# Attention output and decayed receptance transposed by DMA instead of TensorE, in an RWKV-6 and HyperMixer kernel

## The chip, the cores and the metric

The kernel runs on one core of a Trainium2 chip. The metric is the device time of one execution in microseconds; lower is better. Each execution is also put in a state: "slow" when it is over 1.5% above the fastest execution of the same kernel, else "fast". Ratios and their 95% intervals use fast executions alone.

The views name the engines PE (TensorE; PEld are its weight loads), DVE (VectorE), ACT (ScalarE), POOL (GpSimd) and SP (SyncE, which issues most of the DMA transfers here); SPq and ACTq are what SP and ACT issue. In this kernel TensorE writes its products to the memory PSUM, and DVE or ACT copies them out: that copy is an eviction. The granted clock is the share of its full clock that TensorE was given. A transfer is issued, and later it lands.

## The reference

Inputs and output are float32, with B = 4 batches, H = 8 heads, S = 768 positions and D = 48 channels a head. A linear attention with decay feeds a token mixer:

```python
for t in range(S):                       # per batch and head; state is 48 x 48
    cur = einsum('bhd,bhe->bhde', u[None] * k[t], v[t])
    y[t] = einsum('bhd,bhde->bhe', r[t], state + cur)
    state = w[t][..., None] * state + einsum('bhd,bhe->bhde', k[t], v[t])
x = y.transpose(0, 2, 1, 3).reshape(B, S, H * D)          # 4 x 768 x 384
wq, wk = x @ w_q, x @ w_k                                 # 384 -> 64
W_tok = einsum('bsd,btd->bst', wq, wk) / sqrt(64)
mixed = einsum('bst,btd->bsd', W_tok, x)
out = maximum(mixed, 0) @ w_out
```

## The kernel before

The recurrence is done in chunks of 128 positions. A unit `n` is two chunks (256 positions) of one batch; three units make a batch, twelve the problem. For each unit four tensors of 384 KB are loaded. `log`, `sums`, `expk`, `expr` and `decay` make the cumulated decays, `rdec` and `kdec` the decayed receptance Rd and key Kd, with positions on the partitions. For the product of Rd and Kd both are needed with the channels on the partitions: that is the first transposition (`trR`, `evT`). The output Y of a unit is evicted to X, and X is needed transposed for the projections to 64 channels: the second (`xtr`, `xev`). Both run on TensorE, into PSUM, and are evicted by DVE or ACT.

```python
def load(n, nm, ap):                      # ld: a pool of 3 buffers a tensor
    t = ld.tile([C, H, D2], F32, name=nm + "G", tag=nm + "G")
    nc.sync.dma_start(out=t, in_=src.rearrange("h (p j) d -> p h (j d)", j=2))
...
def trR(n, j):                            # j = 0: Rd, 1: Kd
    o = T["psT", n][:, j]
    src = T[("Rd", "Kd")[j], n]
    for hp in range(NP):
        for jj in range(2):
            mm(o[:, :, hp, ds(jj * HC, HC)], src[:, jj, hp], ID128, trans=True)

def evT(n):
    RKT = bt.tile([C, 2, 2, NP, C], BF16, name="RKT", tag="RKT")
    nc.vector.tensor_copy(RKT, T["psT", n])
...
def yst(n):                               # Y += Rd * state
            for hp in range(NP):
                mm(T["Y", n][:, q, ds(hp * D2, D2)], T["RKT", n][:, 0, q, hp],
                   SB[:, ds(hp * D2, D2)], start=False)
...
def xtr(n):
    tp = mtile([128, NK, C2], BF16, "xt_ps")
    for cc in range(2):
        for dt in range(NK):
            mm(tp[:, dt, ds(cc * C, C)],
               T["X", b][:, 2 * m + cc, ds(dt * 128, 128)], ID128, trans=True)

def xev(n):
    copy(ET[n], T["XT", b][:, :, ds(m * C2, C2)], T["tp", n])
...
with tc.manual_schedule():                # each engine gets its work in the order of the plan's times
    for _, _, fn in sorted(plan, key=lambda x: x[:2]):
        fn()
```

Tables such as `EX`, `ET` and `EF` say for each eviction whether ACT (1) or DVE (0) does it, and `ES` whether ACT or SP issues a store. All loads are issued by SP.

Of the kernel before, what the change touches and what calls it, by code (L numbers as in the profile page):

```python
# [12 lines left out]
BF16 = mybir.dt.bfloat16  # L13
# [12 lines left out]
def kernel(  # L26
# [12 lines left out]
    nc = tc.nc  # L39
# [5 lines left out]
    EX = (1, 1, 1, 1, 1, 1, 1, 1, 1, 1, 1, 0)  # L45
    ET = (1, 1, 1, 1, 0, 0, 0, 0, 0, 1, 1, 0)
    EQ = (1, 0, 1, 0, 0, 0, 1, 0, 1, 1, 1, 0)
    EM = (1, 1, 1, 0, 1, 0, 0, 1, 1, 0, 1, 1, 1, 1, 1, 1, 1, 1, 1, 0, 1, 1, 0, 1)
    EF = (0, 1, 0, 1, 1, 1, 1, 0, 0, 1, 1, 0, 1, 1, 1, 1, 1, 1, 0, 0, 0, 0, 0, 0)

    ES = (1, 0, 0, 1, 0, 1, 1, 1, 1, 1, 1, 0, 1, 1, 1, 1, 1, 1, 0, 1, 0, 1, 0, 0)
# [57 lines left out]
    sm = ctx.enter_context(tc.tile_pool(name="sm", bufs=3))  # L109
# [22 lines left out]
    plan = []  # L132

    def at(t, fn):
        plan.append((t, len(plan), fn))



    T = {}
# [6 lines left out]
    def load(n, nm, ap):  # L146
        b, m = divmod(n, NU)
        src = ap[b, :, ds(m * C2, C2)]
        t = ld.tile([C, H, D2], F32, name=nm + "G", tag=nm + "G")
        nc.sync.dma_start(out=t, in_=src.rearrange("h (p j) d -> p h (j d)", j=2))  # L150
        T[nm, n] = t
# [62 lines left out]
    def trR(n, j):  # L214
        T["trR", n, j] = True
        if ("psT", n) not in T:
            T["psT", n] = big([C, 2, 2, NP, C], BF16, "psT")
        o = T["psT", n][:, j]
        src = T[("Rd", "Kd")[j], n]
        for hp in range(NP):  # L220
            for jj in range(2):
                mm(o[:, :, hp, ds(jj * HC, HC)], src[:, jj, hp], ID128, trans=True)

    def evT(n):
        need(("trR", n, 0), ("trR", n, 1))
        RKT = bt.tile([C, 2, 2, NP, C], BF16, name="RKT", tag="RKT")
        nc.vector.tensor_copy(RKT, T["psT", n])  # L227
        T["RKT", n] = RKT

    def amat(n, js):  # L230
        RKT = T["RKT", n]
        A = big([C, 2, NP, C], F32, "A")
        for hp in range(NP):
            for q, hh in ((0, 0), (1, 1), (1, 0), (0, 1)):
                mm(A[ds(q * HC, HC), hh, hp],
                   RKT[ds(hh * 64, D), 1, q, hp, ds(js * HC, HC)],
                   RKT[ds(hh * 64, D), 0, q, hp], start=(hp == 0))
        T["A", n, js] = A
# [80 lines left out]
    def yst(n):  # L319
        T["yst", n] = True  # L320
        b, m = divmod(n, NU)
        for q in range(2):
            if 2 * m + q:
                SB = T["SB", b, 2 * m + q]
                for hp in range(NP):
                    mm(T["Y", n][:, q, ds(hp * D2, D2)], T["RKT", n][:, 0, q, hp],
                       SB[:, ds(hp * D2, D2)], start=False)
# [10 lines left out]
    def yev(n):  # L338
# [3 lines left out]
        if m == 0:  # L342
            T["X", b] = xpool.tile([C, NCH, DM], BF16, name="X", tag="X")
            T["XT", b] = xpool.tile([128, NK, S], BF16, name="XT", tag="XT")
# [3 lines left out]
    def xtr(n):  # L348
        need(("yev", n))
        b, m = divmod(n, NU)  # L350
        tp = mtile([128, NK, C2], BF16, "xt_ps")
        for cc in range(2):
            for dt in range(NK):
                mm(tp[:, dt, ds(cc * C, C)],
# [3 lines left out]
    def xev(n):  # L358
        T["xev", n] = True
        b, m = divmod(n, NU)  # L360
        copy(ET[n], T["XT", b][:, :, ds(m * C2, C2)], T["tp", n])
# [3 lines left out]
    def qkmat(n):  # L365
# [4 lines left out]
        for cc in range(2):  # L370
            for kt in range(NK):
                mm(qk[:, cc], XT[:, kt, ds((2 * m + cc) * C, C)], wk_sb[:, kt],
                   start=(cc == 0 and kt == 0))
        for kt in range(NK):
            for q in range(2):
                mm(qk[ds(q * DH, DH), 2:4].rearrange("p c h -> p (c h)"), T["wq"][:, kt],
                   XT[:, kt, ds((2 * m + q) * C, C)], start=False)
# [46 lines left out]
    def finev(b, c):  # L424
        T["finev", b, c] = True
        if c % 2 == 0:
# [66 lines left out]
    def wcast():  # L493
# [7 lines left out]
    steps = [  # L501
        (-3.67, log, ()),
        (-1.33, uk1, ()),
        (-0.45, sums, ()),
        (-0.42, expk, ()),
        (-0.25, expr, ()),
        (1.36, kdec, ()),
        (1.89, rdec, ()),
        (2.24, decay, ()),
        (3.56, uk2, ()),  # L510
        (5.7, trR, (1, )),
        (5.95, trR, (0, )),
        (5.99, vcast, ()),
        (6.48, red, ()),
        (6.51, vd, ()),
        (7.46, evT, ()),
        (8.59, amat, (0, )),
        (9.91, amat, (1, )),
        (10.1, mask, (0, )),
        (10.73, mask, (1, )),  # L520
        (11.87, state, ()),
        (11.9, stadd, (0, )),
        (12.36, stev, (0, )),
        (13.55, stadd, (1, )),
        (14.38, stev, (1, )),
        (15.25, ymat, ()),
        (15.48, yst, ()),
        (15.48, yd, ()),
        (15.51, yev, ()),
        (17.44, xtr, ()),  # L530
        (18.18, xev, ()),
        (20.45, qkmat, ()),
        (20.75, qkev, ()),
    ]
    first = [
        (-6.23, log, ()),
        (-6.05, sums, ()),
        (-2.68, expk, ()),
        (-0.31, decay, ()),
        (0.59, uk1, ()),  # L540
        (1.7, expr, ()),
        (3.15, kdec, ()),
        (5.93, trR, (1, )),
        (6.95, rdec, ()),
        (6.98, trR, (0, )),
        (7.64, evT, ()),
        (8.73, uk2, ()),
        (9.1, red, ()),
        (9.65, amat, (0, )),
        (9.93, amat, (1, )),  # L550
        (11.0, mask, (0, )),
        (12.22, mask, (1, )),
        (13.97, vcast, ()),
        (14.21, state, ()),
        (14.64, stadd, (0, )),
        (15.85, ymat, ()),
        (16.28, stev, (0, )),
        (16.31, stadd, (1, )),
        (16.31, yst, ()),
        (16.86, stev, (1, )),  # L560
        (16.87, vd, ()),
        (16.9, yd, ()),
        (17.07, yev, ()),
        (18.09, xtr, ()),
        (18.76, xev, ()),
        (20.43, qkmat, ()),
        (20.46, qkev, ()),
    ]
    last = [
        (-8.43, log, ()),  # L570
        (-0.36, sums, ()),
        (-0.33, expk, ()),
        (0.3, expr, ()),
        (0.33, rdec, ()),
        (0.47, decay, ()),
        (1.66, kdec, ()),
        (5.38, vcast, ()),
        (6.06, uk1, ()),
        (6.69, trR, (0, )),
        (7.03, trR, (1, )),  # L580
        (7.36, evT, ()),
        (7.73, uk2, ()),
        (9.43, amat, (0, )),
        (10.04, amat, (1, )),
        (11.58, state, ()),
        (13.51, red, ()),
        (14.13, mask, (0, )),
        (15.69, stadd, (0, )),
        (15.84, vd, ()),
        (15.86, mask, (1, )),  # L590
        (16.87, stev, (0, )),
        (17.84, ymat, ()),
        (17.87, yst, ()),
        (17.87, yd, ()),
        (21.51, stadd, (1, )),
        (29.8, yev, ()),
        (29.83, xtr, ()),
        (33.23, xev, ()),
        (33.26, qkmat, ()),
        (33.29, qkev, ()),  # L600
        (35.83, stev, (1, )),
    ]
    bsteps = [
        (-0.2, tmat, (0, )),
        (-0.17, tmat, (1, )),
        (0.03, tmat, (2, )),
        (0.67, tev, ()),
        (1.72, mix, (0, )),
        (1.75, mixev, (0, 0, )),
        (1.75, mixev, (0, 1, )),  # L610
        (3.02, mix, (1, )),
        (3.05, mixev, (1, 0, )),
        (3.05, mixev, (1, 1, )),
        (5.18, mix, (2, )),
        (5.5, mixev, (2, 0, )),
        (6.82, mixev, (2, 1, )),
        (7.09, fin, (0, )),
        (8.59, fin, (1, )),
        (8.71, fin, (2, )),
        (9.55, finev, (0, )),  # L620
        (9.58, finev, (1, )),
        (12.6, finev, (2, )),
        (13.11, store, (0, )),
        (13.4, fin, (3, )),
        (13.43, finev, (3, )),
        (15.19, store, (1, )),
        (15.4, fin, (4, )),
        (16.51, fin, (5, )),
        (16.54, finev, (4, )),
        (19.42, finev, (5, )),  # L630
        (19.68, store, (2, )),
    ]
    blast = [
        (12.66, tmat, (0, )),
        (12.96, tmat, (1, )),
        (13.44, tmat, (2, )),
        (13.55, tev, ()),
        (13.58, mix, (0, )),
        (14.09, mix, (1, )),
        (14.09, mix, (2, )),  # L640
        (14.12, mixev, (0, 0, )),
        (14.12, mixev, (0, 1, )),
        (14.12, mixev, (1, 0, )),
        (14.12, mixev, (2, 0, )),
        (14.63, mixev, (1, 1, )),
        (28.34, mixev, (2, 1, )),
        (28.37, fin, (0, )),
        (28.5, fin, (1, )),
        (29.14, fin, (2, )),
        (29.18, fin, (3, )),  # L650
        (29.23, finev, (0, )),
        (29.26, finev, (1, )),
        (29.73, store, (0, )),
        (29.74, fin, (4, )),
        (30.7, finev, (2, )),
        (31.09, finev, (3, )),
        (31.34, fin, (5, )),
        (33.84, store, (1, )),
        (34.01, finev, (4, )),
        (35.33, finev, (5, )),  # L660
        (35.36, store, (2, )),
    ]
    start = [0.42, 8.84, 16.14, 23.73, 31.34, 38.86, 46.52, 54.11, 61.53, 69.25, 76.58, 84.42]
    bstart = [40.55, 65.17, 85.94, 114.26]
# [48 lines left out]
```

## Time and profile before

| before | |
|---|---|
| time | 123.33 us, median of 3 executions (122.84 to 123.74) |
| span of the profiled execution | 122.0 us |
| X evicted, units 0, 3 and 11 | at 24.5, 45.6 and 106.5 us |
| POOL ends | 102.2 us |

The prediction below shows the views that say what bounds this kernel.

### The profile page before, as it was taken

How to read it: one execution, taken by the hardware profiler on the slowest of the kernel's cores; microseconds unless marked ns; L12 is line 12 of the kernel's file. 1: busy time of each engine (PE TensorE's matmuls, PEld its weight loads, DVE VectorE, ACT ScalarE, POOL GpSimd, SP SyncE). 2: the span in 40 equal slices, each digit the busy share in tenths (PEclk: the TensorE clock that was granted, in tenths of full speed). 3: DMA queues.
4: the chain of work that ended last, by engine and by line, in shares of the span. 5: the costliest groups of instructions: out<-in, count | busy, mean ns of one | idle time of the engine just before them, and what ended most of it. 6: DMA issues, size and time to landing. Idle time of an engine off the chain costs nothing.

```text
span 122.0 us, 4284 instructions
## 1 busy us (share of the span) xinstructions
PE 100.1 (82%) x1822; PEld 64.6 (53%) x1822; DVE 91.8 (75%) x150; ACT 77.2 (63%) x146; POOL 84.7 (69%) x81
## 2 busy tenths in 40 slices
PE   0193938979898999999999899999999999966800
PEld 0133536557575766757657466576576666532400
DVE  6213596699798978999989998989989777253800
ACT  4236391689779868986685948976478966426000
POOL 8949899995999999599597995967839804000000
PEclk9999996799999999999999999999999999999985
DMA  3999999999999999899839999500552200573092
GB/s 77 322 325 325 323 320 341 292 232 318 236 256 273 288 300 263 230 266 247 245 75 329 348 269 252 149 0 0 134 129 52 82 5 0 129 181 85 24 283 83
DMA packets 54598, 24.66 MB, mean 202 GB/s; under 512 B 51121, under 2 KB 54578, under 8 KB 54578
## 3 DMA queue, kind: packets, MB, share of 16 engines
q1 hardware_dynamic: 52274, 21.24, 64.6%
q10 hardware_dynamic: 2304, 3.15, 9.1%
q8 instruction: 14, 0.23, 0.7%
q14 instruction: 6, 0.05, 0.1%
HBM read 19.66 MB, written 4.72 MB: 200 GB/s over the span
## 4 chain that ended last, share of the span: by engine, by line
PE 68%; ACT 12%; DVE 6%; DMA 3%; POOL 3%; issue 2%; ACTq 1%; SPq 1%; DVEq 0%
PE cw L66 12%; PE Y L66 11%; PE psT L66 10%; PE fps L66 10%; PE Sn L66 5%; PE A L66 5%; PE xt_ps L66 5%; PE qk L66 5%; PE Tps L66 4%; ACT X L130 3%; DMA u<-in_u_dram 3%; DVE AmB L244 3%; ACT XT L130 2%; PE mps L66 2%; POOL uk L250 1%
## 5 line engine op out<-in xcount | busy, mean ns | idle before, releaser
L244 DVE TENSOR_TENSOR AmB<-A,MASK 128x1024 bf16<-128x1024 f32 x24 | 28.8, 1219 | 1.3 <-PE A L66 1.2
L271 POOL TENSOR_TENSOR Vd<-V,diag 128x768 bf16<-128x768 bf16 x12 | 17.7, 1478 | 13.7 <-ACT X L130 3.4
L250 POOL TENSOR_TENSOR uk<-kG,ubc 128x768 f32<-128x768 f32 x12 | 21.8, 1816 | 1.7 <-DVE ubc L486 1.7
L178 ACT ACTIVATE em<-cw,bias 128x384 bf16<-128x384 f32 x24 | 13.0, 580 | 15.6 <-PE cw L66 15.6
L257 POOL TENSOR_TENSOR uk<-uk,rG 128x768 f32<-128x768 f32 x12 | 21.8, 1816 | 0.1
L207 POOL TENSOR_TENSOR KdS<-kG,em 128x768 bf16<-128x768 f32 x12 | 19.7, 1640 | 1.2 <-ACT em L178 1.2
L227 DVE COPY RKT<-psT 128x2048 bf16<-128x2048 bf16 x12 | 14.6, 1217 | 4.0 <-PE psT L66 4.0
L66 PEld LDWEIGHTS <-KdS 64*128 64x128 bf16 (+1 forms) x256 | 10.8, 99 | 9.1 <-POOL KdS L207 3.6
L200 DVE TENSOR_TENSOR RdS<-rG,cw 128x384 bf16<-128x384 f32 x24 | 12.2, 551 | 4.5 <-ACT cw L185 4.5
L66 PE MATMUL fps<-wout_sb,mixT 128*128 128x384 bf16 x72 | 14.6, 328 | 0.1
L302 DVE TENSOR_TENSOR SB<-Sn,pt 128x384 bf16<-128x384 f32 x20 | 11.0, 551 | 4.0 <-PE Sn L66 2.6
L66 PEld LDWEIGHTS <-RKT 48*64 48x64 bf16 (+1 forms) x464 | 10.3, 107 | 7.1 <-issue 4.5
L185 ACT ACTIVATE cw<-cw,bias 128x384 f32<-128x384 f32 x24 | 12.3, 553 | 0.2
L264 DVE TENSOR_REDUCE diag<-uk 128x16 f32<-128x768 f32 x12 | 11.3, 945 | 0.4 <-POOL uk L257 0.4
L155 ACT ACTIVATE logw<-wG 128x768 bf16<-128x768 f32 x12 | 10.2, 851 | 2.1 <-DMA wG<-in_w_dram 2.1
L66 PE MATMUL cw<-logw,BI 128*128 128x384 bf16 x36 | 11.5, 377 | 0.0
L66 PE MATMUL psT<-ID,KdS 128*128 128x128 bf16 x96 | 7.8, 227 | 4.0 <-DVE AmB L244 2.0
L66 PE MATMUL cw<-logw,BS 128*128 128x384 bf16 x36 | 11.0, 363 | 0.0
L66 PE MATMUL A<-RKT 48*64 48x128 bf16 x384 | 10.1, 226 | 0.8 <-ACT X L130 0.8
L130 ACT CAST X<-Y 128x768 bf16<-128x768 f32 x11 | 8.8, 800 | 2.9 <-PE Y L66 2.7
L211 ACT CAST V<-vG 128x768 bf16<-128x768 f32 x12 | 10.0, 841 | 0.0
L130 ACT COPY osb<-fps 128x384 f32<-128x384 f32 x13 | 6.1, 484 | 5.3 <-PE fps L66 2.1
(74 smaller groups left out, 165.1 us busy)
## 6 DMA issues: line engine op xcount, KB each, us to landing
wG<-in_w_dram SPq DMA_DIRECT2D x12, 384.0 KB, 5.5
kG<-in_k_dram SPq DMA_DIRECT2D x12, 384.0 KB, 5.1
rG<-in_r_dram SPq DMA_DIRECT2D x12, 384.0 KB, 4.8
vG<-in_v_dram SPq DMA_DIRECT2D x12, 384.0 KB, 4.9
out_dram<-osb ACTq DMA_DIRECT2D x16, 192.0 KB, 3.0
out_dram<-osb SPq DMA_DIRECT2D x8, 192.0 KB, 3.8
wout_f<-in_moe_w_out_dram SPq DMA_DIRECT2D x1, 576.0 KB, 4.7
wq_f<-in_moe_w_q_dram SPq DMA_DIRECT2D x1, 96.0 KB, 4.1
```

The costliest lines, as they stand in the source:

```text
L66: nc.tensor.matmul(o, l, rr, start=start, stop=stop, skip_group_check=True, is_transpose=trans)
L130: (nc.scalar.copy if e else nc.vector.tensor_copy)(o, i)
L178: nc.scalar.activation(em[:, j], T["cw", n, 1 + j][:, 0:DM], ACT.Exp, bias=bias[2 + j], scale=-1.0)
L185: nc.scalar.activation(cw, cw, ACT.Exp, bias=bias[j], scale=1.0)
L200: nc.vector.tensor_tensor(pad(Rd)[:, j], jhd(T["r", n])[:, j], T["cw", n, j][:, 0:DM].rearrange("p (h d) -> p h d", d=D), ALU.mult)
L207: nc.gpsimd.tensor_tensor(pad(T["Kd", n]), jhd(T["k", n]), hd(T["em", n]), ALU.mult)
L227: nc.vector.tensor_copy(RKT, T["psT", n])
L244: nc.vector.tensor_tensor(T["AmB", n][:, js].rearrange("p q h t -> p h q t"), T["A", n, js], _rep(_rep(MASK[:, js], 1, NP), 1, 2), ALU.mult)
L250: nc.gpsimd.tensor_tensor(uk, T["k", n].rearrange("p h (j d) -> p h j d", j=2), _rep(ubc.rearrange("p (h d) -> p h d", d=D), 2, 2), ALU.mult)
L257: nc.gpsimd.tensor_tensor(uk, uk, T["r", n].rearrange("p h (j d) -> p h j d", j=2), ALU.mult)
L264: nc.vector.tensor_reduce(diag.rearrange("p j h -> p h j"), T["uk", n], axis=AX.X, op=ALU.add)
L271: nc.gpsimd.tensor_tensor(Vd, T["V2", n], _rep(T["diag", n], 3, D), ALU.mult)
```

## The change

The intent is to take the transposition of Rd (but of the first unit) and of X (but of the last) off TensorE, which sets the pace, and to let the DMA queue of SP do it, straight from SBUF to SBUF, without PSUM and without an eviction. With it come another layout of the transposed tiles, a product of Rd and state split into two column halves, other choices of engines for evictions, 21 of the 24 stores on SP in place of 8, and one explicit table of steps in place of the plan sorted by times.

```diff
-    EX = (1, 1, 1, 1, 1, 1, 1, 1, 1, 1, 1, 0)
+    EX = (0, 1, 0, 1, 1, 1, 1, 1, 1, 0, 1, 1)
 ...                                        # ET, EQ, EM, EF likewise
-    ES = (1, 0, 0, 1, 0, 1, 1, 1, 1, 1, 1, 0, 1, 1, 1, 1, 1, 1, 0, 1, 0, 1, 0, 0)
+    ES = (0, 0, 0, 0, 0, 0, 0, 0, 0, 0, 0, 0, 0, 0, 0, 0, 0, 0, 0, 1, 0, 1, 0, 1)
+    DT = (1, 1, 1, 1, 1, 1, 1, 1, 1, 1, 1, 0)
+    DR = (0, 1, 1, 1, 1, 1, 1, 1, 1, 1, 1, 1)
-    sm = ctx.enter_context(tc.tile_pool(name="sm", bufs=3))
+    sm = ctx.enter_context(tc.tile_pool(name="sm", bufs=5))
 ...
+    def trR(n, a):
+        if a == 0 and DR[n]:
+            T["RT", n] = bt.tile([C, 2, NP, C], BF16, name="RT", tag="RT")
+            nc.sync.dma_start_transpose(
+                out=T["RT", n].rearrange("p j q t -> p (j q) t"),
+                in_=src.rearrange("p j q d -> p (j q d)"))
+            return
 ...
     def evT(n):
+        if DR[n]:
+            T["KT", n] = bt.tile([C, 2, NP, C], BF16, name="KT", tag="KT")
+            nc.vector.tensor_copy(T["KT", n], T["psT", n])
 ...
     def yst(n):
-                    mm(T["Y", n][:, q, ds(hp * D2, D2)], T["RKT", n][:, 0, q, hp],
-                       SB[:, ds(hp * D2, D2)], start=False)
+                    for j in range(2):
+                        mm(T["Y", n][ds(j * HC, HC), q, ds(hp * D2, D2)],
+                           T["RT", n][:, j, hp, ds(q * HC, HC)], SB[:, ds(hp * D2, D2)],
+                           start=False)
 ...
     def xtr(n):
+        if DT[n]:
+            nc.sync.dma_start_transpose(
+                out=T["XT", b][:, ds(2 * m, 2)].rearrange("p c k t -> p (c k) t"),
+                in_=T["X", b][:, ds(2 * m, 2)].rearrange("p c d -> p (c d)"))
+            return
 ...
-        for _, _, fn in sorted(plan, key=lambda x: x[:2]):
-            fn()
+    order = (
+        (load, 0, "w"), (load, 0, "k"), (uload,), (load, 0, "r"), (load, 0, "v"),
 ...                                        # some 540 steps
+        for fn, *a in order:
+            fn(*a)
```

## The prediction

> **What bounds the kernel now.** I read the page's busy line first, then the busy time by stretches, then the chain of waits, then the groups of instructions, then the DMA rows.
>
> The busy line of the page (share of the span, number of instructions):
>
> ```profile
> PE 100.1 (82%) x1822; PEld 64.6 (53%) x1822; DVE 91.8 (75%) x150; ACT 77.2 (63%) x146; POOL 84.7 (69%) x81
> ```
>
> It shows four engines between 63% and 82%. An average over the span does not name a bound, so I asked for four stretches (columns: stretch, its length, busy PE, PEld, DVE, ACT, POOL, granted clock, DMA share, GB/s):
>
> ```profile
> 0.00:20.00 20.00, 10.05 (x104) 6.00 (x104) 10.67 (x37) 9.71 (x16) 16.83 (x40) 0.98 1.03 288
> 20.00:35.00 15.00, 13.41 (x275) 9.26 (x272) 12.16 (x17) 11.41 (x22) 13.52 (x10) 0.91 1.03 270
> 35.00:105.00 70.00, 68.31 (x1349) 45.00 (x1348) 62.82 (x87) 52.58 (x102) 54.36 (x33) 1.00 0.66 178
> 105.00:122.00 17.00, 8.37 (x102) 4.31 (x101) 6.16 (x12) 3.46 (x8) 0.00 (x0) 0.89 0.51 141
> ```
>
> From 35 to 105 us TensorE is busy 68.3 of 70 us (98%) at full clock, DVE 90%, POOL 78%, ACT 75%. TensorE sets the pace there. The chain of waits says the same: it is 68% TensorE, and between 56 and 66 us it never leaves TensorE. One unit of 256 positions in it (start, us, what):
>
> ```profile
> 57.48 1.00 PE psT L66 x16
> 58.48 1.20 PE cw L66 x15
> 59.68 0.62 PE fps L66 x3
> 60.30 1.39 PE Y L66 x44
> ...
> 62.62 0.46 PE xt_ps L66 x6
> ...
> 65.05 1.00 PE psT L66 x16
> ```
>
> The same work comes back after 65.05 - 57.48 = 7.57 us: that is the period of a unit. Of it, 1.00 us are the 16 transposes of Rd and Kd and 0.46 us the 6 transposes of X. The groups that the change touches (busy us, mean ns of one):
>
> ```profile
> L66 PE MATMUL psT<-ID,RdS 128*128 128x128 bf16 x96 | 8.2, 235 | 0.0
> L66 PE MATMUL xt_ps<-ID,X 128*128 128x128 bf16 x72 | 6.1, 221 | 2.1 <-ACT X L130 1.6 <-ACT osb L130 0.5
> L66 PE MATMUL Y<-SB,RKT 128*128 128x96 bf16 x80 | 5.5, 208 | 0.0
> L227 DVE COPY RKT<-psT 128x2048 bf16<-128x2048 bf16 x12 | 14.6, 1217 | 4.0 <-PE psT L66 4.0
> L130 ACT COPY XT<-xt_ps 128x768 bf16<-128x768 bf16 x6 | 4.8, 799 | 2.1 <-PE xt_ps L66 2.1
> ```
>
> The DMA rows (40 slices of 3.05 us) show full queues in the first 57 us, at 320 to 325 GB/s early on, and room after that:
>
> ```profile
> DMA  3999999999999999899839999500552200573092
> q1 hardware_dynamic: 52274, 21.24, 64.6%
> ```
>
> **What the Trainium skill says.** "DMA: Bandwidth & Descriptors", section "Latency and other measured facts", gives a DMA transpose 261 GB/s as measured in one kernel with a non-contiguous middle dimension and some 350 to 400 GB/s when contiguous. There is no DMA transpose in the trace of before, so nothing here confirms it; this is the figure on which most of my risk hangs. "VectorE: DVE Perf Modes", section "The three transpose paths", has 390 ns for a 128x128 on TensorE (into PSUM, to be evicted) and 1309 ns for the DMA (straight into SBUF). The trace has 221 to 235 ns for one on TensorE, and pipelined 6 take 0.46 us, so 77 ns each. The DMA path is thus the slower one per tile, and pays only because it runs beside TensorE. "TensorEngine Tiling (Array Packing)", section "Tiling Modes", says that tiles on separate column halves can load and multiply in parallel. The trace agrees: 12 matmuls of 384 columns with 64-wide weights (Tps) take 1.10 us in the chain, 92 ns each, against 0.59 us for 3 with 128-wide weights (fps), 197 ns each. "DMA: Bandwidth & Descriptors", section "Issuing engines are not separate DMA queues", says that moving a DMA between issuing engines saves sequencer time only. In the trace one store issued by ACT holds it 0.60 to 0.63 us.
>
> **The change part by part.**
>
> Rd transposed by DMA (11 of 12 units). It takes 88 transposes off TensorE: half of the psT piece, 0.50 us per unit on the path, 5.5 us in all. The DVE copy from PSUM shrinks from 2048 to 1024 columns: about 0.61 of 1.22 us, 11 times, 6.7 us of DVE (estimate, by proportion).
>
> X transposed by DMA (11 of 12). It takes 66 transposes off TensorE, 0.46 us per unit on the path, 5.1 us in all, and the evictions of XT: 6 of 0.80 us from ACT, 5 of 0.55 us from DVE. The last unit stays on TensorE, so the tail keeps its short path.
>
> Added on TensorE: the product of R and the state is split into column halves, 160 matmuls in place of 80, with the halves alternating. Eight took 0.45 us in the pipeline. If the halves overlap as Tps shows, sixteen take the same; if weight loads hold them to some 48 ns each (the wq matmuls, 6 in 0.29 us), 0.77 us. I take +0.1 us per unit, about 1 us in all.
>
> TensorE on the path: 5.5 + 5.1 - 1 = 9.6 us off. The period becomes 7.57 - 0.96 + 0.1 = 6.7 us.
>
> Added on the SP queue: 11 transposes of 256 KB and 11 of 192 KB, 5.05 MB. At 261 GB/s that is 19 us of queue time (estimate from the skill's figure). Loads are 48 x 393,216 B, 1.21 us each at 325 GB/s, which agrees with the 1.15 to 1.23 us between load issues in the trace: 58 us, plus 2.4 us for the weights. Per unit: 4.8 us of loads and about 1.75 us of transposes, 6.6 us. This just fits in 6.7, and only until the loads end; the stores then have the queue. All loads are issued before the first store, and each transpose stands one to two units ahead of its reader in the table, so its latency is covered.
>
> Evictions and stores: by the instruction counts of the two kernels DVE loses 9 of 11 osb copies, all 6 qk copies, and gains 2 X copies and a mixT; with the parts above it goes from 91.8 to about 77.6 us. ACT gains 9 osb and 6 qk copies and loses 6 XT and 2 X: 77.2 to about 76.8 us, and 13 of its 16 store issues at 0.6 us leave, 8 us of its sequencer. POOL keeps the same 48 instructions: 21.8 + 21.8 + 19.7 + 17.7 = 81.0 us, 6.75 us per unit.
>
> Sum: TensorE wants 6.7, POOL 6.75, ACT 6.4, DVE 6.5 and the SP queue 6.6 us per unit. After the change five resources are level, so I expect some 80% of the 9.6 us: 7.7 us. The first matmuls no longer stand behind the product that waits for u (5.53 to 7.08 us in the timeline), which may give a little; the last evictions all on ACT with its stores between may cost as much. 123.3 - 7.8 = 115.5 us.
>
> **The rivals.**
>
> First, POOL becomes the bound. It works on uk, kdec and Vd from 7.8 us on, and 81.0 us without a gap ends at 88.8; before, it idled 13.7 us ahead of Vd and ended at 102.2, 20 us before the end. For it: 6.75 against 6.7 us. Against it: this is hardly longer than TensorE's own period. It would give 111 to 116 us, the centre of my range.
>
> Second, the SP queue becomes the bound. A transpose waits in it for its source, and every load behind it waits too; and if the transposes ran at half the skill's rate, a unit would want 4.8 + 3.5 = 8.3 us until the loads end. That is over the old 7.57 us: the time would be 122 to 132 us. For it: the queue is full for 57 us already, and no transpose has been measured here. Against it: loads run ahead by three buffers, and from 60 us on the queue has room.
>
> Third, the new order alone does the work, or spoils it. The table moves evictions and whole steps, so it may take out the 3 to 4 us of waits of DVE and POOL in the middle (109 to 112 us), or leave gaps if it was tuned on wrong DMA times (118 to 123 us).
>
> **Range and chances.** The path argument gives 113.7 us if all 9.6 us come through and 118 to 119 if half do. I widen below to 109 for the order and above to 123 for the queue. Faster by over 2% means under 120.9 us: 0.77. Within 2%: 0.12. Slower, which needs the second rival in strength: 0.11.
>
> **What would show it.** Right: TensorE's busy time near 89 us, DVE near 78, a chain in which psT pieces are half as long and xt_ps nearly gone, a unit period of 6.7 to 7.1 us in the middle, POOL over 85% busy there. The Y piece should stay within 1.4 to 1.7 us. Transposes should land within about 5 us of issue, in the queue with the loads. Wrong: waits of TensorE weight loads or matmuls on DMA into RT or XT; ACT or POOL waiting for loads; transposes with more than 2 us of queue time each; a middle stretch with TensorE under 85% busy though its work shrank; or a tail longer than the 14.5 us that before needs from the last transposes of X to its end.

## More of the kernel before

From the page, the TensorE clock that was granted in each of 40 slices, in tenths of full speed:

```profile
PEclk9999996799999999999999999999999999999985
```

The reader sees full clock nearly everywhere, apart from two slices early and the end. From the timeline of the DMA queue of SP, the last load (start, length of the issue, queue, line, operation):

```profile
74.28 0.37 SPq L150 DMA_DIRECT2D vG<-in_v_dram  x1
```

All loads have been issued at 74.3 us, 32 us before the last X. And from the view by stretches, the middle of the kernel in one line (columns as in the prediction: stretch, length, busy PE, PEld, DVE, ACT and POOL with the number of instructions, granted clock, DMA share, GB/s):

```profile
25.00:90.00 65.00, 62.00 (x1256) 42.13 (x1256) 60.53 (x84) 50.44 (x96) 54.70 (x34) 1.00 0.84 225
```

## The result, and the profile after

| | before | after |
|---|---|---|
| time, median of 4 executions | 123.53 us | 143.92 us (142.78 to 145.14) |
| ratio after/before of fast executions | | 1.163, 95% interval 1.154 to 1.172 |
| X evicted, units 0, 3 and 11 | 24.5, 45.6, 106.5 us | 22.9, 58.2, 127.2 us |
| POOL ends | 102.2 us | 120.0 us |

A ratio is the mean time of one kernel's fast runs over that of the other's from the same rounds, so it is not quite the ratio of the medians. The changed kernel is correct, and 16% slower. The profiled execution of it, from which the lines below come, is the longest of the four, 145.14 us; its granted clock was 0.83 and that of the three fast ones (142.78 to 144.05 us) 0.84 to 0.86.

The page of the kernel after, its busy line, clock, DMA share by slice (3.6 us each) and the row of the DMA queue (packets, MB, share of the span of 16 engines):

```profile
PE 101.9 (71%) x1748; PEld 62.8 (44%) x1748; DVE 80.2 (56%) x133; ACT 78.4 (55%) x152; POOL 84.8 (59%) x81
...
PEclk9999779655559955998569999789659999999985
DMA  4999999999999999999989989999800065666565
...
q1 hardware_dynamic: 74562, 28.84, 89.3%
```

No engine is over 71% busy, while the DMA engines are nearly full for the first 104 us (29 slices): with the same loads and stores, the queue has gone from 64.6% to 89.3% of a longer span. TensorE runs 74 matmuls fewer and yet is busier (101.9 us against 100.1), while its clock falls again and again. The middle stretch, against the line of before above:

```profile
25.00:90.00 65.00, 46.86 (x865) 29.78 (x864) 39.73 (x52) 38.08 (x74) 47.56 (x30) 0.76 1.13 238
```

Of 65 us TensorE works 46.9, at a mean clock of 0.76. What the engines wait for (engine and line, what ended the wait, us in total, times, longest):

```profile
...
PEld L70 <- DMA RT<-RdS: 18.7, 6, 5.5
PE A L70 <- DMA RT<-RdS: 17.3, 7, 5.1
...
ACT logw L155 <- DMA wG<-in_w_dram: 12.6, 8, 2.2
...
POOL uk L265 <- DMA kG<-in_k_dram: 9.7, 5, 2.8
...
DVE RdS L200 <- DMA rG<-in_r_dram: 7.8, 2, 4.2
```

Every engine waits for DMA: TensorE for the transposed Rd (the first two lines are one stall seen from the weight loads and from the matmuls), ACT, POOL and DVE for loads. So the transposes come late and the loads too. The landing of a transpose after its issue, from the DMA rows (last column, median us), is not the reason:

```profile
RT<-RdS SPq DMA_TRANSPOSE x11, 4.8
XT<-X SPq DMA_TRANSPOSE x11, 3.5
```

These are no longer than the loads' 4.6 to 5.6 us. The reason shows in the timeline of SP's queue:

```profile
44.22 1.16 SPq L150 DMA_DIRECT2D vG<-in_v_dram  x1
45.47 2.63 SPq L220 DMA_TRANSPOSE RT<-RdS  x1
48.19 0.53 SPq L150 DMA_DIRECT2D wG<-in_w_dram  x1
...
52.30 1.99 SPq L369 DMA_TRANSPOSE XT<-X  x1
54.38 2.15 SPq L220 DMA_TRANSPOSE RT<-RdS  x1
...
77.29 3.87 SPq L220 DMA_TRANSPOSE RT<-RdS  x1
81.25 1.24 SPq L369 DMA_TRANSPOSE XT<-X  x1
...
89.73 0.53 SPq L150 DMA_DIRECT2D rG<-in_r_dram  x1
```

A transpose holds SP for 1.2 to 3.9 us, where 1.0 us is what the prediction's rate gives for the larger of the two, and the last load goes out at 89.7 us, not at 74. From the first transpose (25.7 us) to the last load SP issued 30 loads and 14 transposes in 64.6 us, and the 14 held it for 34.4 us. These lengths can't be shared out one by one, since a load right behind a transpose often holds SP for 0.53 us only. But thirty loads at the 1.21 us of before are 36.3 us; so by difference the transposes took some 2.0 us each (an estimate), and a unit (four loads, two transposes) 64.6 / 7.5 = 8.6 us of queue, above the old period of 7.57. In the chain that ended last, which reaches back to 87.8 us only, TensorE stands three times for a landing (start, us, what):

```profile
98.51 4.25 DMA XT<-X
102.76 0.05 issue
102.81 1.85 PE qk L70 x23
...
114.47 4.58 DMA RT<-RdS
```

The third is 2.90 us at 87.8 us. This is one half of the second rival of the prediction, slow transposes in a full queue. Its other half, a transpose that waits for its source and holds the loads behind it, the timelines do not show: up to the last load SP is idle for no more than 0.1 us before any of the 14 transposes, and every source was written 7 to 16 us before the issue (that of the one at 77.29 us by 67.8 us). But the change also brought a new order, other evictions and stores, and what is said above is a reading of one trace. The experiments take it apart.

### The profile page after: what moved, and what is told of

The parts are those of the page before. It is cut to its first block, busy times and chain, and to the rows that moved or that the text cites. A ratio compares the mean times of both kernels' runs of the same rounds, so it can differ in the third digit from the quotient of the medians.

```text
span 143.4 us, 4200 instructions
## 1 busy us (share of the span) xinstructions
PE 101.9 (71%) x1748; PEld 62.8 (44%) x1748; DVE 80.2 (56%) x133; ACT 78.4 (55%) x152; POOL 84.8 (59%) x81
## 3 DMA queue, kind: packets, MB, share of 16 engines
q1 hardware_dynamic: 74562, 28.84, 89.3%
## 5 line engine op out<-in xcount | busy, mean ns | idle before, releaser
L70 PE MATMUL A<-RT,KT 48*64 48x128 bf16 x352 | 10.8, 262 | 18.1 <-DMA RT<-RdS 17.3
L286 POOL TENSOR_TENSOR Vd<-V,diag 128x768 bf16<-128x768 bf16 x12 | 17.6, 1473 | 9.9 <-DVE diag L279 9.3
L70 PE MATMUL cw<-logw,BI 128*128 128x384 bf16 x36 | 12.9, 419 | 7.2 <-ACT logw L155 7.2
L70 PEld LDWEIGHTS <-KT 48*64 48x64 bf16 x352 | 7.3, 130 | 23.6 <-DMA RT<-RdS 18.7
L70 PEld LDWEIGHTS <-KdS 64*128 64x128 bf16 (+1 forms) x256 | 13.2, 114 | 7.5 <-issue 3.8
L134 ACT COPY osb<-fps 128x384 f32<-128x384 f32 x22 | 10.3, 479 | 9.8 <-PE fps L70 7.4
L70 PE MATMUL fps<-wout_sb,mixT 128*128 128x384 bf16 x72 | 14.1, 328 | 0.4
L70 PE MATMUL cw<-logw,BS 128*128 128x384 bf16 x36 | 12.7, 415 | 0.0
L239 DVE COPY KT<-psK 128x1024 bf16<-128x1024 bf16 x11 | 7.6, 689 | 8.5 <-PE psK L70 8.2
L435 ACT ACTIVATE mixT<-mps 128x384 bf16<-128x384 f32 x17 | 7.7, 490 | 4.9 <-PE mps L70 4.8
L134 ACT CAST qks<-qk 128x256 bf16<-128x256 f32 x12 | 4.5, 372 | 10.6 <-PE qk L70 10.6
```

What stands on the lines that cost most here:

```text
L70: nc.tensor.matmul(o, l, rr, start=start, stop=stop, skip_group_check=True, is_transpose=trans)
L134: (nc.scalar.copy if e else nc.vector.tensor_copy)(o, i)
L286: nc.gpsimd.tensor_tensor(Vd, T["V2", n], _rep(T["diag", n], 3, D), ALU.mult)
```

## The experiments

The theories: **Q**, the queue: a transpose takes much more time of the DMA queue than a copy of its size, loads and transposes come late, and engines wait. **O**, the order: the table of steps or the code's other changes cost the time. **L**, latency: a reader stands too close behind its transpose. **W**, head of line: a transpose waits in SP's queue for its source and holds the loads behind it.

### The disputed cost by itself

The kernel before, with bursts appended behind its last store: 24 transposes (12 of 256 KB, 12 of 192 KB), 12 copies of 256 KB from SBUF to SBUF, 12 loads, and 12 pairs of a load and a transpose.

```diff
+        for i in range(12): tr(i, 8)       # dma_start_transpose of 8 blocks of 128x128
+        for i in range(12): tr(i, 6)
+        for i in range(12): cp(i)          # dma_start, the same 256 KB
+        for i in range(12): ldw(i)         # load of w, 384 KB
+        for i in range(12): ldw(i); tr(i, 8)
```

> The kernel before, with five groups of 12 extra DMAs on the SP queue after its last store: 256 KB transposes, 192 KB transposes, plain 256 KB copies inside SBUF, 384 KB loads, and 12 pairs of a load and a 256 KB transpose. Theory 'slow transposes' (a transpose holds the 16 DMA engines for more than twice what its bytes would take): once the queue is full, 2.2 to 2.6 us between 256 KB transposes, 1.6 to 2.0 us between 192 KB ones, 0.8 us between plain copies, 1.2 us between loads, 3.4 to 3.8 us for a pair. Rival 'skill's rate' (the queue was slow only because transposes waited for their sources in it): 1.0, 0.75, 0.8, 1.2 and 2.2 us. A third, 'turning the queue round' (mixing loads with transposes costs extra): 1.0 us in the burst but well over 3 us for a pair.

The timeline of SP in that kernel:

```profile
117.26 33.46 SPq L687 DMA_TRANSPOSE scr<-RdS  x24
150.76 7.79 SPq L689 DMA_DIRECT2D scr<-RdS  x12
...
179.96 1.69 SPq L687 DMA_TRANSPOSE scr<-RdS  x1
181.69 0.58 SPq L691 DMA_DIRECT2D lds<-in_w_dram  x1
```

A transpose takes 33.46 / 24 = 1.39 us on average, 5.5 MB in 33.46 us or 165 GB/s; the copy of 256 KB 7.79 / 12 = 0.65 us. A pair took 2.53 us, about what a load (1.2 to 1.36 us) and a transpose take one after the other, so that in a burst mixing costs nothing extra. My expectations of 1.0 us and of 2.2 to 2.6 us both missed: the truth lies between. With 2.8 us of transposes a unit wants at least 4.8 + 2.8 = 7.6 us of queue, the old period.

A second burst took other sizes: 8 transposes each of 256, 192, 128, 64 and 32 KB, with four copies of 256 KB between them.

```diff
+        for m in (8, 6, 4, 2, 1):          # blocks of 128x128 (32 KB)
+            for i in range(8): tr(i, m)
+            for i in range(4): cp(i)
```

> The kernel before, with bursts of 8 DMA transposes of 256, 192, 128, 64 and 32 KB after its last store, 4 plain copies between bursts. The first burst had 1.36 us for 256 KB and 1.33 us for 192 KB, hardly different. Theory 'floor' (issuing one transpose takes about 1.2 us whatever its size): 1.2 to 1.36 us for all five sizes. Rival 'bytes': 1.36, 1.1, 0.7, 0.4 and 0.3 us or so, with the 192 KB of the first burst an exception.

The timeline of SP, for 256 KB, a set of copies, then 64 and 32 KB:

```profile
118.16 11.63 SPq L686 DMA_TRANSPOSE scr<-RdS  x8
129.84 2.53 SPq L688 DMA_DIRECT2D scr<-RdS  x4
...
158.83 10.29 SPq L686 DMA_TRANSPOSE scr<-RdS  x8
...
171.75 10.19 SPq L686 DMA_TRANSPOSE scr<-RdS  x8
```

That is 1.45, 1.29 and 1.27 us for one (192 and 128 KB, not shown: 1.34 and 1.31). Eight times the bytes cost 14% more: alone in the queue, no transpose took less than 1.27 us on average. But the view by stretches of the same run gives a DMA share of 1.03 (engines full), 0.83, 0.59, 0.36 and 0.25 for the five sizes: a small transpose holds SP as long, yet leaves most of the DMA engines' time free.

### The changed kernel with the transposes back on TensorE (inconclusive)

Three kernels keep the table of steps and set `DT`, `DR` or both to zero; the transposes then stand on TensorE right before their evictions.

```diff
-    DT = (1, 1, 1, 1, 1, 1, 1, 1, 1, 1, 1, 0)
+    DT = (0, 0, 0, 0, 0, 0, 0, 0, 0, 0, 0, 0)     # both; likewise DR
+    # in the order: xtr moved to just before xev, trR to just before evT
```

> The changed kernel with its order of steps, its stores on SP and its evictions, but with all 22 DMA transposes back on TensorE (those of X right before their eviction, those of Rd and Kd right before the copy out of PSUM). Theory 'queue' (the DMA transposes are what costs, by the queue time and latency they bring): back to 119 to 128 us, TensorE's granted clock back over 0.93. Rival 'order' (the new order of steps, stores and evictions is what is slow): stays at 137 us or more.

> As the run without DMA transposes, but X alone by DMA (11 of 12 units). Theory 'queue': 6 transposes of 192 KB lie ahead of the last loads, 11 to 12 us of queue time at 1.8 us each, part of it slack: 125 to 134 us, between none and both. Rival 'order': 137 us or more, as with none. Rival 'Rd alone is to blame' (a long transpose that waits in the queue for DVE): within 2 us of none.

> As the run without DMA transposes, but Rd alone by DMA (11 of 12 units). Theory 'queue': 8 transposes of 256 KB lie ahead of the last loads, 19 us of queue time at 2.4 us each: 130 to 140 us, slower than X alone. Rival 'order': 137 us or more in all three of these runs. Rival 'X alone is to blame': within 2 us of none.

Neither by DMA (e1_none): 152.2 us (ratio 1.216, 1.207 to 1.224). X alone by DMA (e2_xonly): 142.91 (1.157, 1.149 to 1.164). Rd alone (e3_ronly): 138.8 (1.122, 1.117 to 1.128). The waits of the first say why it was so slow:

```profile
DVE RKT L242 <- PE psT L70: 20.1, 12, 3.4
...
DVE XT L134 <- PE xt_ps L70: 7.9, 9, 2.3
```

By putting a transpose right in front of its eviction I made DVE stand for TensorE, 12 times for RKT alone. These runs measure my rewriting and say nothing on the order or on the DMA.

### The changed kernel with the transposes made cheap

Three kernels keep the changed code, the table of steps and every wait, and make the transposes or the loads cheap. Their outputs are wrong, which doesn't matter for the times. The first replaces each transpose by a copy of 4 KB, from the same source to a tile of the same place in the chain:

```diff
-            nc.sync.dma_start_transpose(out=T["RT", n]..., in_=src...)
+            nc.sync.dma_start(out=T["RT", n][0:16, 0, 0], in_=src[0:16, 0, 0])
```

> The changed kernel, same order and same waits, but each DMA transpose is replaced by a 4 KB copy from the same source into a static tile (wrong results on purpose): no volume in the queue, shorter latency. Theory 'queue and latency': the waits of TensorE for RT and XT go from 17 and 4 us to under 3 us, loads end before 75 us, the time is 112 to 122 us. Rival 'order' (steps, stores and evictions are what is slow, as the 152 us without DMA transposes suggest): 132 us or more, with the clock still under 0.92.

The second keeps the real transposes and loads only the first three units, so that the queue has room:

```diff
     def load(n, nm):
+        if n >= 3:
+            T[nm, n] = T[nm, n % 3]
+            return
```

> The changed kernel with its transposes as they are, but loads for units 0 to 2 only, whose data all later units use again (wrong results on purpose): the queue carries transposes and stores alone. Theory 'queue' (transposes and loads together fill it): 112 to 124 us, transposes landing in about 3 us. Rival 'latency and order' (TensorE stands in its order before data that are not yet there, whatever the load on the queue): 130 us or more.

The third replaces each transpose by a plain copy of the same bytes, to the same tile:

```diff
-            nc.sync.dma_start_transpose(out=...rearrange("p j q t -> p (j q) t"), in_=...)
+            nc.sync.dma_start(out=...rearrange("p j q t -> p (j q t)"), in_=...)
```

> The changed kernel with each DMA transpose replaced by a plain copy of the same bytes to the same tile (wrong results on purpose). In the burst a plain 256 KB copy took 0.65 us of the queue and a transpose 1.36. Theory 'the transposing is dear' (a transpose holds the queue twice as long as its bytes): 125 to 133 us. Rival 'bytes' (any 5 MB more in this queue costs the same): 140 us or more.

| kernel | median us | ratio to before (95%) | start to X of unit 3 | from there to X of unit 11 | after the last X |
|---|---|---|---|---|---|
| before | 123.33 | | 45.6 | 60.9 | 15.5 |
| after | 143.92 | 1.163 (1.154 to 1.172) | 58.2 | 69.0 | 16.2 |
| copies of 4 KB (e4_tiny) | 123.48 | 0.989 (0.983 to 0.995) | 52.5 | 53.1 | 16.8 |
| loads of 3 units alone (e5_noload) | 125.41 | 1.014 (1.009 to 1.019) | 51.5 | 53.9 | 17.6 |
| copies of the same bytes (e6_copy) | 125.74 | 1.010 (1.001 to 1.019) | 50.6 | 56.2 | 16.7 |

The last three columns split the span of each profiled execution at the eviction of X of units 3 and 11. (The profiled executions of after and of the 4 KB copies were slow ones, the others fast.) Of the four executions of the same-bytes copies two are fast, 125.23 and 124.10 us; the other two, 126.24 and 126.48, count as slow.

The copy of the same bytes decides. It has the order, the bytes, the waits and about the landing time of the changed kernel, but it doesn't transpose. Its middle stretch, with the columns as before:

```profile
25.00:90.00 65.00, 51.38 (x1153) 33.83 (x1152) 47.89 (x65) 44.59 (x88) 59.90 (x37) 0.95 0.98 281
```

Its last load, from the timeline of SP:

```profile
74.06 0.77 SPq L150 DMA_DIRECT2D rG<-in_r_dram  x1
```

The landings of its copies, from the DMA rows:

```profile
RT<-RdS SPq DMA_DIRECT2D x11, 256.0 KB, 4.7
XT<-X SPq DMA_DIRECT2D x11, 192.0 KB, 4.1
```

The loads end at 74.1 us in place of 89.7, the clock is back at 0.95, and POOL works 59.9 of 65 us in place of 47.6. In fast executions after is at 143.5 us on average and this at 124.7: 18.9 of the some 20 us lost are the transposing itself. For the changed kernel O, as the main cause, is out, and so is L, since these copies land no sooner than the transposes did (4.7 and 4.1 us against 4.8 and 3.5).

With the loads away, the transposes are paid and cost little: 125.2 us in fast executions, against 122.6 with copies of 4 KB and the loads. The middle stretch of the kernel with the loads of three units:

```profile
25.00:90.00 65.00, 55.80 (x1206) 36.64 (x1206) 50.47 (x68) 45.30 (x90) 60.14 (x38) 0.90 0.47 82
```

TensorE is down to 55.8 of 65 us, and POOL at 60.1 (93%) is the busiest: the first rival of the prediction, once the queue is free. From unit 3 to unit 11 it takes 53.9 us against 60.9 of before, 6.7 us a unit in place of 7.6: the predicted gain in the middle is there (predicted: 6.7 in place of 7.57). But the table of steps gives it back. In all three kernels X of unit 3 comes 5 to 7 us later than before, and the tail is 1 to 2 us longer. The two sums nearly cancel. So even with cheap transposes the changed kernel doesn't beat the one before by 2%. The traces place the delay between X of unit 0 and X of unit 1, 12.5 to 13.4 us apart in the three and 7.3 before; what in the new order causes it was not taken apart.

### The kernel before with transposes by DMA

The other direction: the changed code, but with the plan, the evictions and the stores of before. The loads are placed where their buffers come free. The base has no transposes by DMA; in the others Rd is transposed right behind `rdec` and `qkmat` comes later.

```diff
-    DT = (1, 1, 1, 1, 1, 1, 1, 1, 1, 1, 1, 0)
-    DR = (0, 1, 1, 1, 1, 1, 1, 1, 1, 1, 1, 1)
+    DT = (0, ...)                              # o_none; o_r sets DR, o_x_lag DT,
+    DR = (0, ...)                              # o_rx and o_rx_lag both, o_late units 7 on
-    order = (...)                              # the table out, the plan of before in
+            at(t, lambda n=n, nm=nm: load(n, nm))
+            if fn is trR and a == (0,) and DR[n]:
+                dt = (1.9 if n < NT - 1 else 0.34)
+            if fn in (qkmat, qkev) and DT[n]:
+                dt += 3.0                      # o_rx; o_late 3.3 from unit 6 on; o_x_lag and
+                                               # o_rx_lag 7.6 up to unit 5, with the mixing
+                                               # of batches 0 and 1 7.6 us later
```

> The kernel before's list of timed steps, evictions and store engines in the changed code, no DMA transposes, loads issued in the order of units as their buffers come free. A control for the next runs: 121 to 128 us if the changed code itself (column halves, layout of RT, XT) costs nothing; rival 'changed code costs': over 130 us.

> As the control, but Rd and X both by DMA in 11 of 12 units (the transposes of Rd right after rdec, qk 3 us later for units whose X goes by DMA). Theory 'queue' (7.4 us of loads and transposes per unit by the burst's 1.21, 1.31 and 1.25 us): slower than the control by 5 us or more, though no order table is in it. Rival 'order' (the table is what lost the time and transposes as such are a gain): faster than the control by 5 us or more.

> The control with the kernel before's list of steps, Rd alone by DMA (11 units). The burst gave 1.36 us for a 256 KB transpose and 1.21 us for a load, so the queue wants 4.84 + 1.36 = 6.2 us per unit, less than TensorE's new 7.07 us. Theory 'queue full' (both transposes together are just over what the queue has): 117 to 123 us, no loss. Rival 'any transpose in the load queue hurts' (by the head of the line: it waits for DVE and holds the loads behind it): 127 us or more.

> The control, X alone by DMA (11 units), qk of the first six units and the mixing of the first two batches one unit (7.6 us) later so that the landing of XT is covered. Queue: 4.84 + 1.33 = 6.2 us per unit. Theory 'queue full': 117 to 124 us. Rival 'any transpose in the load queue hurts': 127 us or more.

> Both by DMA, with the same 7.6 us of cover as the run of X alone. Queue: 4.84 + 1.36 + 1.33 = 7.53 us per unit, as long as the old period, at best. Theory 'queue full': 128 to 140 us although landings are covered. Rival 'latency' (the 142 us without cover came from TensorE standing before XT): 117 to 124 us.

> The control, both by DMA for units 7 to 10 (and Rd of 11) alone, whose transposes come when the last loads are being issued or are done. Theory 'queue full': 119 to 123 us, at most 4 x 0.96 us gained. Rival 'latency': 125 us or more, as TensorE has only 3 us of cover for XT.

| kernel | transposes by DMA | median us | ratio to before (95%) |
|---|---|---|---|
| o_none | 0 | 123.06 | 0.997 (0.993 to 1.001) |
| o_late, units 7 on | 9 | 130.04 | 1.050 (1.045 to 1.056) |
| o_r, Rd alone | 11 | 132.61 | 1.061 (1.053 to 1.070) |
| o_x_lag, X alone | 11 | 133.76 | 1.081 (1.075 to 1.087) |
| o_rx, both | 22 | 141.91 | 1.146 (1.137 to 1.154) |
| o_rx_lag, both, read later | 22 | 143.98 | 1.161 (1.149 to 1.172) |

The base settles that the changed code costs nothing by itself: layouts, split product and all, it runs as before. Without the table of steps both transposes cost as much as with it: 141.9 against 143.9 us. Giving the readers of X more time in the first units (o_rx_lag) did not help: 144.0 us, where I had expected 128 to 140. And I had expected the kernels with half of the transposes, or with transposes only where the queue has room, to lose nothing or to gain (117 to 124 us). They lost 6.2 us (o_late), 7.6 (o_r) and 10.0 (o_x_lag) in fast executions.

The evictions of X in the traces say where, and it is not in step with the number of transposes. In o_late X of unit 6 comes at 68.8 us (base 68.7), of unit 7 at 84.2 (77.2), of unit 11 at 113.3 (106.4): the whole loss is one stop, in which TensorE waits 5.8 us for the first Rd from the DMA. Its source was written at 62.1 us, and it was issued at 70.0, behind two loads, the first of which was issued only at 66.1, and two stores. In o_x_lag X of unit 7 still comes at 76.3 us (base 77.2), although seven transposes went out among the loads; the 10 us go after it, where the readers have 3.0 us more only and the mixing that I had put off is done. That fits late landings and places in the queue better than a queue that is too full, but no run took them apart. L, which is out for the changed kernel, isn't out for these two.

### Cover and the head of the line

In o_r two things can be mixed: late landings, and loads that stand in SP's queue behind a transpose whose source isn't ready. Three kernels do the work from `log` to `rdec` 7.6 us earlier (one period), with a fourth load buffer and more stores on ACT, so that some 14 us lie between a transpose of Rd and its reader.

```diff
-    ld = ctx.enter_context(tc.tile_pool(name="ld", bufs=3))
+    ld = ctx.enter_context(tc.tile_pool(name="ld", bufs=4))
+            if n >= 2 and fn in (log, sums, expk, expr, decay, kdec, rdec) or (
+                    n >= 2 and fn is trR and a == (0,) and DR[n]):
+                dt -= 7.6
```

> A control: the kernel before's steps, log to rdec of units 2 to 11 moved one unit (7.6 us) ahead, a fourth buffer for each load, the stores of the first two batches all on ACT; no DMA transposes. 121 to 129 us if this is harmless.

> The same, with Rd by DMA in 11 units: the transpose has some 14 us from its source to its reader, no store of the first batches stands before it in the queue, and the queue wants 4.84 us of loads and 1.4 to 2.0 us of transpose per unit. Theory 'late landing' (Rd alone cost 9 us only because its landing was not covered): faster than its control by 2 us or more. Rival 'queue': slower than its control by 4 us or more even so.

> The same, with Rd by DMA for units 7 to 11 alone, by when half of the loads have been issued. Theory 'late landing': 1 to 3 us faster than the control. Rival 'queue': as the control or slower.

The control without transposes by DMA (c_none) took 130.38 us (1.059, 1.050 to 1.067), so that my rearrangement itself cost 7 us. With Rd by DMA (c_r) it took 137.74 (1.111, 1.102 to 1.121), and with Rd of units 7 on (c_rlate) 134.8 (1.094, 1.086 to 1.102). TensorE now waits only 1.3 us for the transposed Rd in the kernel with all of Rd by DMA, and still that kernel is 6.5 us above its control in fast executions. Up to X of unit 6 the transposes with cover cost next to nothing, 74.5 us against 74.0 in the control, where o_r, without cover, was 6.1 us behind its base (in a slow execution). The loss comes in units 7 and 8 (X of unit 8 at 97.7 us, control 90.8). With five transposes the loss is 4.4 us. There SP stands 6.0 us before the first of them, until its source is written at 58.6 us, and the four loads that the control issues from 52.8 to 56.9 us go out from 60.1 to 70.1. ACT waits 8.7 us for w against 6.3 in the control. That is W at work. (A longer wait for `RdS`, 9.7 us up to 98.2, comes after the last load at 84.7 and holds none.) But no run of mine took that wait away alone, so W's share of the time stays open; in the changed kernel, as said above, there was no such wait before the last load.

### Half of the bytes

The last kernel is the changed one with each transpose cut to half of its bytes, into tiles of its own, at the same places. Its output is wrong, which doesn't matter for the time.

```diff
-            nc.sync.dma_start_transpose(out=T["RT", n]..., in_=src...)      # 8 blocks
+            nc.sync.dma_start_transpose(out=T["RT", n][:, 0], in_=src[:, 0]...)   # 4 blocks
```

> The changed kernel, each DMA transpose moving half of its bytes into static tiles (wrong results on purpose). Theory 'floor': the queue is held as long as with whole ones: 138 us or more. Rival 'bytes': about half of the 20 us between tiny copies (122 to 123 us) and whole transposes (144 us) remains: 129 to 136 us.

The median is 135.4 us; fast executions took 132.66 and 134.21, 133.4 on average, beside 123.64 for before. So of the 21 us between copies of 4 KB (122.6 us in fast executions) and whole transposes (143.5), 10.9 remain with half of the bytes. The floor of 1.27 us, which I found in the burst, would have left nearly all, had SP's time been what cost. Between loads, then, the cost goes with the bytes, about in proportion. The DMA shares of the burst of sizes suggest how the two fit: alone, SP's time sets the pace, and the engines' time goes with the bytes (share 0.59 for half of them); in the kernel the loads want those engines too. No run shows this apart, nor why a transpose took some 2.0 us there in place of 1.39.

No correct kernel of these is faster than the one before. The base with the old plan equals it (0.997), and the 4 KB copies (0.989) compute nothing of use.

## Why the prediction was wrong

**The bound was right.** TensorE set the pace, and taking the transposes off it frees it: with the queue unloaded it works 55.8 of 65 us in the middle, against 62.0.

**The step that failed** is the queue term: "At 261 GB/s that is 19 us of queue time (estimate from the skill's figure)", and from it "about 1.75 us of transposes, 6.6 us" per unit. The 22 transposes take 22 x 1.39 = 31 us in a burst, and 22 x 2.0 = 44 us at the rate of the stretch between 25.7 and 90.3 us. A unit thus wants 7.6 us at best and 8.6 as it ran, and not 6.6. The second rival had the mechanism in its clause on slow transposes, and even the size (8.3 us a unit), but I gave it 0.11; its other clause, a transpose that waits for its source, was not what happened up to the last load. My error was the rate: I took a figure that nothing in the trace confirmed, and I had the warning beside it, 1309 ns for one 128x128 block, and let it go. The burst has 1.27 us of queue time for that block.

**The rival's own range (122 to 132 us) was too low**, since the lost time is more than the difference in period. Loads and transposes come late together; TensorE stops, and in the middle its granted clock falls to 0.76, so that what it then does takes longer: 101.9 us busy where 92.0 were enough with plain copies and 89 were predicted. The Trainium skill, "TensorE: Matmul & The Clock Gate", section "What's actually happening", tells of a clock that halves after an idle window of some 3.4 us, and the trace agrees in kind: TensorE stops for 4.2 us up to 31.0 us, 5.1 up to 51.3 and 3.5 up to 67.6, and the page shows clocks of 0.5 in slices at or just after each of them, where that of before has full clock. The share of the clock in the 20 us was not measured apart.

**"From 60 us on the queue has room"** failed too. Already the DMA row that the prediction shows is full again in slices 22 to 25 (64 to 76 us), when the last loads of before go. In the changed kernel the loads end at 89.7 us, not at 74, and six stores on SP follow at once, from 90.4 to 95.7 us, with transposes waiting behind them. The kernel with transposes in its last units alone lost 5%, in one stop behind loads and stores.

**"Each transpose stands one to two units ahead of its reader in the table, so its latency is covered"** was right on the latency (4.8 and 3.5 us at the median, "within about 5 us") and wrong on the wait, which came from the place in the queue.

**The terms of the engines held.** DVE's busy time is 80.2 us (predicted 78), ACT's 78.4 (76.8). The smaller copy of the transposed Kd, from the groups of instructions of the kernel after (busy us, mean ns):

```profile
L239 DVE COPY KT<-psK 128x1024 bf16<-128x1024 bf16 x11 | 7.6, 689 | 8.5 <-PE psK L70 8.2
```

It takes 689 ns, where 610 had been estimated by proportion. The column halves overlap: 16 of the split matmuls take 0.53 us in the timeline, where 8 whole ones took 0.51.

**The middle gain was right, the order was not foreseen.** Once transposes are cheap or the loads gone, the eight units from 3 to 11 take 6.6 to 7.0 us each, where the path argument had 6.7, and POOL is the next bound, as the first rival had it. But the table of steps loses 5 to 7 us in the first four units and 1 to 2 in the tail. So the third rival ("or spoils it") holds for the ends. So 115.5 us would not have come about had the queue term been right: the three kernels with cheap transposes or few loads took 122.6 to 125.2 us in fast executions, at or past the upper end of the range. (The last sum takes 7.8 us off where 7.7 had been worked out; it changes nothing.)

## What to carry to other kernels

Before moving transposes from TensorE to DMA, time a dozen of them in a burst behind the kernel, in the size and the queue that they will use, and add them to the loads of one period: here 1.4 us each, twice the copy of the same bytes, was enough to close a queue that was full already. To separate an operation from its bytes, its waits and its order, replace it by a plain copy of the same bytes between the same tiles; that one run told more than the twelve that rearranged the schedule. And a new control must equal the old kernel before anything is read off it: two of my three did not.

## What the Trainium skill lacked or had wrong

- "DMA: Bandwidth & Descriptors", section "Latency and other measured facts", gives transposes by DMA 261 GB/s, and 350 to 400 when contiguous. Between SBUF tiles, in a burst, the runs show 165 GB/s for 256 and 192 KB together, and 26 GB/s for 32 KB (32,768 bytes in 1.27 us). In the kernel, among loads, a transpose of 192 to 256 KB took about 2.0 us (an estimate by difference).
- "Advanced Engine Details and Errata", section "X-Bar Transpose (TRN2)", says that "TRN2 transpose DMAs are as fast as regular DMAs". The runs show 1.39 us against 0.65 us, for 224 KB on average and 256 KB.
- "VectorE: DVE Perf Modes", section "The three transpose paths", has 1309 ns for a 128x128 by DMA, and 1.27 us of queue time is close to it. It doesn't say that eight such blocks take hardly longer (1.45 us for 256 KB).
